# Seventeen weight sums from VectorE to GpSimd, with a new hand-written order, in a one-core attention and MLP kernel

## The chip, the cores and the metric

The kernel runs on one core of one Trainium2 chip. The metric is the device time of one execution in microseconds; lower is better. Five engines work beside each other, each through its own queue in order: TensorE (PE; its weight loads are listed as PEld), VectorE (DVE), ScalarE (ACT), GpSimd (POOL) and SyncE (SP), which here issues nearly all DMAs. An engine waits at the head of its queue until the semaphores of its next instruction are met, and everything behind that instruction waits too.

## The reference

Gated linear attention over four sequences of 768 tokens, eight heads of 48, and behind it one MLP block with a layer norm and a residual:

```python
def _attn_ref(q, k, v, alpha):            # (B, H, S, D) = (4, 8, 768, 48)
    for t in range(S):
        state = alpha[:, :, t, :, None] * state + np.einsum('bhd,bhe->bhde', k[:, :, t], v[:, :, t])
        y[:, :, t] = np.einsum('bhd,bhde->bhe', q[:, :, t], state)

def _moe_ref(x, g_ln, w_ch1, w_ch2):      # x is (4, 768, 384), w_ch1 (384, 1536), w_ch2 (1536, 384)
    xn = (x - mu) / np.sqrt(var + 1e-06) * g_ln
    return x + np.maximum(xn @ w_ch1, 0.0) @ w_ch2
```

All is computed in float32; the two weight matrices arrive as 64-bit floats and are turned into float32 on the chip.

## The kernel before

**Tiling.** The 768 tokens are cut into six chunks of 128, with the four sequences beside each other: 24 pieces of attention, each a generator `attention(c, b)`. Chunk 0 goes through the MLP in the plain way: `hidden` (line 561) and `project` (line 573). Chunks 1 to 5 use fast matrix multiplication. The first product xn @ w_ch1 is split into 3 x 3 blocks of the weights and 3 x 2 blocks of the tokens and made from 15 block products instead of 18 (`hidden_product`, line 853); the second from 20 instead of 24 (`product`, line 673). Each block product multiplies a sum of weight blocks by a sum of token blocks. The token side is summed once a chunk (`combine_x`, line 827; `combine_hidden`, line 660), the weight side once in all: `combine_first` for the first weights (line 802, the subject here) and `combine_weights` for the second (line 633).

**Order.** Nothing is scheduled automatically. Every part of the work is a Python generator, named by one character, and the string `ORDER` (lines 28 to 48, 1501 characters) says whose next step is emitted:

```python
for turn in ORDER:
    next(turns[turn], None)
```

Since each engine runs its queue in order, `ORDER` fixes on each engine what stands behind what. The characters that matter here: `a` to `x` are the 24 attention pieces (`a` is chunk 0, sequence 0); `0` to `3` issue the loads of alpha, k, q and v on SP; `A` to `L` load and convert the twelve weight pieces; `Y`, `Z`, `P`, `Q` are the MLP of chunk 0; `S` is `combine_first` (26 turns), `W` `combine_weights`, `X` `combine_x`, `N` `combine_hidden`, `M` and `V` the block products, `R` the relus, `O` the reloads of what is added at the end.

**combine_first.** Its first nine turns scale nine of the twelve blocks of w1 by the layer norm's gain, on ScalarE (line 779). Then follow 17 sums and differences of blocks, 17 turns, made with `add` and `sub` of line 786. A block is 128 x 512 float32. Two of the results are held as two halves of 128 x 256 in spare room, so these two take two instructions each, and two more halves make 19 instructions: 15 of 128 x 512 and 4 of 128 x 256. Results go to `ready`, from which `hidden_product` takes its weights; the block products of a chunk go in the order `FIRST = (11, 3, 7, 5, 10, 9, 1, 4, 14, 6, 13, 2, 8, 0, 12)`, and the first of them needs the twelfth of the 17 sums.

**What else stands on DVE and GpSimd.** On DVE: the conversion of weights (lines 223 to 233, with line 229 on ScalarE), q and k times their decay (line 309; the q form reads two SBUF tiles, the k form one SBUF tile and PSUM), masks (line 380), state updates (line 409), sums of the second weights (line 633), of tokens (827) and hidden blocks (660), and the sums that take block products out of PSUM (863 to 896 and 683 to 731). On GpSimd: causal masks of chunk 0 (line 377), the gate on the state (line 411, which follows line 409 and is waited for by the attention outputs of line 437), and late sums of the two fast products (lines 872, 875, 878, 879, 888, 891, 892, and 689).

**Attention's start.** A piece takes the logarithm of alpha (line 293, ScalarE), sums it with a triangular matmul (298, or 522 for later chunks), takes exponentials (303, 304), multiplies q and k (309), transposes them (325 or 346), and goes on to scores (366, 538), state updates (396) and outputs (421, 437); then come the norm (453 to 480) and its transposes (487, 503).

Of the kernel before, what the change touches and what calls it, by code (L numbers as in the profile page):

```python
# [25 lines left out]


ORDER = (
    "0aa0bb00c2211dd2a3a2aabbbcaaacbbb0bd1a1abbbdfa1dddaaa3bbbec4aac2cd0baaafdAcbe2cc"
    "ffebdddccccdebb31eg0abhAffffeeecA4gdddccA5fdggheddeeeccYYiYhBjfcfhdgeeecggdchhhg"  # L30
    "hBB1ZZZfffB3CCZAefffe5hghB4fCjYYYYYiZZZCYYZZDD2jji3YYiDjjjhiiEZZZC0kDYYY3hhhZEig"
    "FFE5iggjGlF4ZZZZZgglS1lEHYYYhhghHjYYGYYhZZ2llgll3jHZFYGjHkkZkgI0kk0kjjjYZZnKI3i3"
    "ImQSSiiGii4n2jj1jSj5IlkkkkJKSSSSl1feeJn2eKeJLLnhL0hi02jSmPSPSjjmmQ1PPKSSSPkffPP1"
    "fnhPhSmkSWWSQ2SmmSefefWgnggnhQphSogSilllS5n3mimnggXXlXXX33WQQQ0nnXQXk4ppXXomSlll"
    "lnMMpmMoonMMMMMM2MMWSSkk0XSXlmmnnnmmMmMMM3MM13MnMnooppMMMoMMMMWpkrRM0M5poqooo4iq"
    "WWjjMMMMiMMRWMMMpooRiRMMMWMMoMMMlMMOOM1rrr22MMMRRqipMpoiikWMMMMRRMRMMMnnppokMMMM"
    "MRRRNNp3nMONlNlp0nnpWOqtrrmmNWNrN0MMNMMMMMNkNMMMMNN3MMsMMMMMmq0pNlpq1q3kMNOMlkMN"
    "MMMM5XXXXXrrrqq4MqqNXt1XoMMMMMMXXsstqqproM2MrrrJMMuvpoMMMMMMXMMMMMMXsMMMMMtMMrMo"
    "stssMMMqMtMtMM52rrsttssm4ssstMRttMMMMtt1MrMOOMMMMrMvMO2MMMMRRRvRMMMMMMMRRMMRMMML"
    "u31uMMRMRMMssNqNNNvrsmu22RNNNNNRqqNNNNm001MpMMMMMMMMMMM3MMMMMMMMMMMMNMMMrppNoNuv"  # L40
    "vMMoMMMMMXXX3MMM1XXvuu5vuuXvwXXvx4twuuvvqqMXXOOuMMsttttOMMMMMMMMMMXMMMwtMMMMwMMM"
    "33txxxMMMMMMMRqMMMMMMMMMMMMMMMussMsruuwrxRRRMMMMMRRRMRxMMRMMMMwwMMMMMMvxvvvvv5xx"
    "xwwwwwNNRONRRNttqqMMNNxMMMMMxNvMMMMMMMMNNNNNwwxsvMvwwMMxsMMuNNMMXXxNNxxxXXMXXXMM"
    "MXMMMMMXOMMMxMMXXMMMMMMMMMMwwOOuMMMMMMMMMMMMMMMMMMMMMMMMMMMRRRMMMMMMMMMMMROMxwuR"
    "uuwMMMMMMMMMMRRRRNRMMRRMMNMNNMNNNNMMMMMMMMMMMxNMNNXXXXXXMMMXNNMMMMMMNNNMMVVVVVVX"
    "MMMXXXMMMMMMMMVVVVVVVVOOOMOVVVVVVVVVVVVVVVRRRRRVVVVVVVVVRVVVVVVVVVVVVVVVVVVVVVVR"
    "RRNNRNRMMNRNNNMMMNNNMMMMNNNMMMMMMMMMMMMMMMMMMMNNMMMMNMMMMMMMM"
)


# [1 line left out]
def kernel(  # L52
# [36 lines left out]
    nc = tc.nc  # L89
# [670 lines left out]
    def first_weights_ready():  # L760
        if "a" not in first_of:
            first_of["a"] = {n: [w1[:, 2 * t:2 * t + 2, f]]
                             for n, t, f in ((7, 2, 1), (10, 1, 0), (13, 0, 1), (8, 0, 0))}
        return first_of["a"]
# [11 lines left out]
    def combine_first():  # L776
        a = [[w1[:, 2 * t:2 * t + 2, f]] for t in range(3) for f in range(NF)]
        for n in (3, 7, 5, 8, 1, 4, 0, 2, 6):
            nc.scalar.mul(a[n][0], a[n][0], g_col[:, n % NF:n % NF + 1])
            yield  # L780
        extra = cpool.tile([P, 6 * P], FP32, name="extra")
        spare = [raw.tile([P, 2, 2, NP, D], FP32, name=f"r{n}", tag="in", bufs=6).rearrange(
            "t b i p d -> t (b i p d)") for n in "akq"] + [extra]
        n3, n5, n0, n11 = ([x[:, :4 * P].rearrange("p (a c) -> p a c", a=2)] for x in spare)
        n9, n1 = ([x[:, 4 * P:].unsqueeze(1) for x in spare[2 * i:2 * i + 2]] for i in range(2))
        add, sub = nc.vector.tensor_add, nc.vector.tensor_sub
        ready = first_weights_ready()

        def parts(x, n):
            return x if len(x) == n else [x[0][:, :1], x[0][:, 1:]]  # L790

        for n, op, out, x, y in (
                (3, sub, n3, a[3], a[7]), (5, add, n5, n3, a[5]), (9, add, n9, n3, a[8]),
                (None, sub, n0, a[1], a[3]), (1, sub, n1, n0, a[5]), (0, sub, n0, n0, a[4]),
                (None, sub, a[4], a[3], a[4]), (4, add, a[4], a[4], a[5]),
                (None, sub, a[5], a[0], a[7]), (None, sub, n11, a[2], a[8]),
                (14, add, a[8], a[5], a[8]), (11, sub, n11, n11, n5),
                (12, sub, a[5], a[5], a[6]), (None, sub, a[6], a[8], a[5]),
                (6, sub, a[6], a[6], a[7]), (None, add, a[2], a[2], a[0]),
                (2, sub, a[2], a[2], a[1])):  # L800
            for o, u, w in zip(out, parts(x, len(out)), parts(y, len(out))):
                op(o, u, w)
            if n is not None:
                ready[n] = out
            yield
# [117 lines left out]
    def second_of_chunk_0(h):  # L923
        for i in range(3):
            for b in range(2 * h, 2 * h + 2):
# [6 lines left out]
    turns |= {chr(ord("a") + n): attention(n // B, n % B) for n in range(NCB * B)}  # L932
    turns |= {chr(ord("A") + i): take_weights(i) for i in range(len(pieces))}
    turns |= {"M": mlp(), "V": hidden_products(NCB - 1), "S": combine_first(), "W": combine_weights(), "R": relus(),
              "X": (x for c in range(1, NCB) for x in combine_x(c)),
              "N": (x for c in range(1, NCB) for x in combine_hidden(c)), "O": outputs()}
# [32 lines left out]
```

## Time and profile before

| what | value |
|---|---|
| median of 3 runs | 425.02 us (424.80 to 425.43) |
| the profiled execution | 425.22 us |
| its span on the engines | 423.5 us |
| TensorE clock granted | 0.999 |
| GpSimd busy from 80 to 100 us, from 100 to 120 us | 2.03 us, 1.91 us |
| DVE busy in the same stretches | 18.15 us, 18.54 us |
| DVE busy from 400 to 420 us | 15.17 us |

The span is what the engines' records cover; the 1.7 us that the execution took beyond it lie around it. A row of a source view gives the line, engine, operation, tiles and count, then the shortest, median and longest duration in ns, the first and last start in us, and the shapes. A row of the view of waits reads: who waited and for whom, then us in total, how often, and the longest. A piece of the chain of waits gives its start, its length and what it was; matmuls are counted there by records, and a float32 matmul leaves two.

### The profile page before, as it was taken

The page shows a single profiled execution, that of the slowest core. Times are in us where ns is not written, and L with a number is a line of the kernel's source. Part 1 is how long each engine was busy: PE and PEld are TensorE (multiplying, and loading weights), DVE is VectorE, ACT ScalarE, POOL GpSimd, SP SyncE. Part 2 cuts the span into 40 slices and gives each one's busy share as a digit, 9 for nine tenths or more (in the row PEclk, how much of TensorE's full clock was granted, in tenths as well). Part 3 has the DMA queues.
Part 4 walks back from the last instruction along what each step waited for, and adds up shares of the span by engine and source line. Part 5 has one row for each costly group of instructions (what it writes and reads, how often), then busy time and mean ns, then how long its engine had stood idle before and what let it go on. Part 6 is the DMA issues. An engine that isn't in the chain of part 4 may idle for free.

```text
span 423.5 us, 14136 instructions
## 1 busy us (share of the span) xinstructions
PE 416.2 (98%) x5988; PEld 366.9 (87%) x5988; DVE 327.2 (77%) x626; ACT 228.1 (54%) x572; POOL 155.0 (37%) x181
## 2 busy tenths in 40 slices
PE   8989999999999999999999999999999999999997
PEld 6878778766778889998889998899998899988996
DVE  4688889898998988878678667749676679756684
ACT  6986577969634879434666066486432551114200
POOL 3242010110125491244771333771145650656414
PEclk9999999999999999999999999999999999999999
DMA  7989766783534341161513226002122000130001
GB/s 241 245 199 285 252 167 197 235 248 116 116 96 134 97 131 60 36 176 38 137 36 104 68 83 165 2 22 39 35 83 74 2 2 0 39 112 2 0 18 58
DMA packets 51095, 43.95 MB, mean 104 GB/s; under 512 B 23468, under 2 KB 47148, under 8 KB 51032
## 3 DMA queue, kind: packets, MB, share of 16 engines
q1 hardware_dynamic: 50632, 43.04, 35.5%
q8 instruction: 47, 0.77, 0.8%
q14 instruction: 16, 0.13, 0.1%
q10 hardware_dynamic: 400, 0.00, 0.1%
HBM read 34.29 MB, written 8.74 MB: 102 GB/s over the span
## 4 chain that ended last, share of the span: by engine, by line
PE 89%; ACT 3%; DVE 3%; DMA 2%; issue 1%; SPq 1%; DVEq 0%; ACTq 0%
PE ops L673 31%; PE hps L853 31%; PE ops L573 7%; PE hps L561 6%; PE yps L437 5%; PE aps L538 2%; PE tps L346 2%; PE ups L396 2%; DMA vx<-in_v_dram 1%; PE lps L522 1%; DMA ra<-in_alpha_dram 1%; PE tps L325 1%; PE xps L503 1%; DVE qk L309 1%; ACT qT L332 1%
## 5 line engine op out<-in xcount | busy, mean ns | idle before, releaser
L689 POOL TENSOR_TENSOR ob<-ob,u 128x192 f32<-128x192 f32 x40 | 25.4, 646 | 88.4 <-DVE ob L686 66.1
L853 PE MATMUL hps<-sum,w 128*128 128x256 f32 x192 | 47.5, 382 | 0.1
L411 POOL TENSOR_TENSOR mid<-mid,gate 112x192 f32<-112x192 f32 x20 | 11.4, 571 | 91.9 <-DVE mid L409 55.7
L853 PEld LDWEIGHTS hps<-sum,w 128*128 128x128 f32 x192 | 36.1, 190 | 5.1 <-DVE qk L309 0.2
L673 PE MATMUL ops<-w,hT 128*128 128x192 f32 x224 | 39.9, 327 | 0.0
L673 PEld LDWEIGHTS ops<-w,hT 128*128 128x128 f32 x224 | 36.9, 190 | 0.3
L561 PE MATMUL hps<-xT,w 128*128 128x256 f32 x144 | 33.5, 385 | 1.0 <-issue 0.9
L853 PE MATMUL hps<-xT,w 128*128 128x256 f32 x136 | 34.4, 380 | 0.0
L561 PEld LDWEIGHTS hps<-xT,w 128*128 128x128 f32 x144 | 26.6, 190 | 6.3 <-ACT lps L304 1.1
L573 PE MATMUL ops<-w,hT 128*128 128x384 f32 x96 | 32.0, 488 | 0.0
L904 ACT ACTIVATE hT<-hT 128x512 f32<-128x512 f32 x48 | 27.3, 628 | 7.9 <-POOL hT L891 2.7
L853 PEld LDWEIGHTS hps<-xT,w 128*128 128x128 f32 x136 | 25.8, 190 | 3.5
L673 PE MATMUL ops<-ws,sum 128*128 128x192 f32 x160 | 28.6, 327 | 0.0
L573 PEld LDWEIGHTS ops<-w,hT 128*128 128x128 f32 x96 | 17.9, 190 | 11.5
L683 DVE TENSOR_TENSOR ob<-ops,ob 128x192 f32<-128x192 f32 x50 | 17.1, 352 | 13.0 <-PE ops L673 7.6
L673 PEld LDWEIGHTS ops<-ws,sum 128*128 128x128 f32 x160 | 26.4, 190 | 0.0
L356 ACT COPY qT<-tps 112x512 uint16<-112x512 uint16 x32 | 17.2, 602 | 16.1 <-PE tps L346 16.0
L673 PE MATMUL ops<-ws,hT 128*128 128x192 f32 x128 | 23.4, 326 | 0.0
L507 ACT COPY xT<-xps 128x384 uint16<-128x384 uint16 x32 | 13.5, 492 | 16.9 <-PE xps L503 16.9
L673 PE MATMUL ops<-more,sum 128*128 128x192 f32 x120 | 22.2, 328 | 0.0
L673 PEld LDWEIGHTS ops<-ws,hT 128*128 128x128 f32 x128 | 21.3, 190 | 0.1
L437 PE MATMUL yps<-mid,qT 48*64 48x48 f32 x320 | 21.0, 220 | 0.0
(253 smaller groups left out, 1139.8 us busy)
## 6 DMA issues: line engine op xcount, KB each, us to landing
ws<-in_moe_w_ch_dram SPq DMA_DIRECT2D x12, 768.0 KB
vn<-in_v_dram SPq DMA_DIRECT2D x12, 384.0 KB
kept<-x SPq DMA_DIRECT2D x20, 192.0 KB
ob<-kept SPq DMA_DIRECT2D x20, 192.0 KB
out_dram<-ob SPq DMA_DIRECT2D x19, 192.0 KB
ra<-in_alpha_dram SPq DMA_DIRECT2D x18, 192.0 KB
rq<-in_q_dram SPq DMA_DIRECT2D x16, 192.0 KB
rk<-in_k_dram SPq DMA_DIRECT2D x16, 192.0 KB
```

The lines of the kernel that those rows point to most:

```text
L346: nc.tensor.transpose(tv[cs, n, p, w], words[halves[h], n, p, i, :cs.stop - cs.start, w], ident_of_halves[halves[h]])
L356: nc.scalar.copy(out=to, in_=tps[h].bitcast(UINT16).rearrange("r (n p w t) -> r n p t w", n=2, p=NP, w=2)[:R, n])
L411: nc.gpsimd.tensor_mul(new, new, by)
L437: nc.tensor.matmul(yps[r][halves[s], i, p], of, by, start=not (odd and inner), stop=bool(inner or not odd), skip_group_check=bool(odd))
L507: nc.scalar.copy(out=xT_of[c][:, :, b, halves[h]].bitcast(UINT16).rearrange("r f (t w) -> r f t w", w=2), in_=xps[h].bitcast(UINT16)[:, :2 ...
L561: nc.tensor.matmul(hps, w1[:, j // 2, f, j % 2 * P:][:, :P], xT_of[0][:, f, bs], start=(f == 0), stop=(f == NF - 1))
L573: nc.tensor.matmul(ops_of[b], hT_of[c][:, j, b], w2[:, j], start=(j == 0), stop=(j == NJ - 1))
L673: nc.tensor.matmul(acc, lhs[:, j], rhs[:, j], start=(j == 0), stop=(j == NT - 1))
L683: nc.vector.tensor_add(x, acc, x)
L689: getattr(nc.gpsimd, f"tensor_{op}")(x, x, y)
L853: nc.tensor.matmul(acc[:, i], w, b, start=True, stop=True)
L904: nc.scalar.activation(out=x, in_=x, func=AFT.Relu)
```

## The change

In `combine_first` the two operations of line 786 are taken from GpSimd instead of VectorE; all 17 sums, 19 instructions, follow. `ORDER` is replaced as a whole: the same 1501 characters in another sequence, with every generator taking as many turns as before. TensorE's 3742 matmul instructions are the same ones in another order.

```diff
 ORDER = (
-    "0aa0bb00c2211dd2a3a2aabbbcaaacbbb0bd1a1abbbdfa1dddaaa3bbbec4aac2cd0baaafdAcbe2cc"
+    "0aa000bcbca2211d0aabdcaaabbbdba3fbbeaa122bb4ccaade1aa1dbbbfaccccad2ddedabbf3bcAc"
...
-    "fnhPhSmkSWWSQ2SmmSefefWgnggnhQphSogSilllS5n3mimnggXXlXXX33WQQQ0nnXQXk4ppXXomSlll"
-    "lnMMpmMoonMMMMMM2MMWSSkk0XSXlmmnnnmmMmMMM3MM13MnMnooppMMMoMMMMWpkrRM0M5poqooo4iq"
+    "memmhPWSSWffQ0g2gWQWi0mn5ngnim3hgQSSghX1XSSSlXXX2XXXXQQQmlnllnnmXlnlpo4pop1loMol"
+    "MMSlSMMMMMMkjjSSMMMpjjMmmMMMSkkjpXmmjMMW3W3ppMMMmmMooMMRMoMMMMnnmnn5ooooMM0MMMnn"
...
 )

-        add, sub = nc.vector.tensor_add, nc.vector.tensor_sub
+        add, sub = nc.gpsimd.tensor_add, nc.gpsimd.tensor_sub
         ready = first_weights_ready()
```

The other lines of `ORDER` differ as much. In the new order the first seven of the 19 instructions stand on GpSimd behind the state update of st_0_105, the next seven behind one more update, then come three updates and four sums around the update of st_0_109, and the last stands behind the first sums of the fast product (lines 872 and 875). On ScalarE the first exponential (line 303) now stands behind the third logarithm (line 293), where before it stood behind the fourth.

More of the change, by code (lines that the diff above doesn't have):

```diff
@@ L28 @@
 ORDER = (
-    "0aa0bb00c2211dd2a3a2aabbbcaaacbbb0bd1a1abbbdfa1dddaaa3bbbec4aac2cd0baaafdAcbe2cc"
[L30 to L33, printed above, removed]
-    "fnhPhSmkSWWSQ2SmmSefefWgnggnhQphSogSilllS5n3mimnggXXlXXX33WQQQ0nnXQXk4ppXXomSlll"
@@ L35 @@
-    "lnMMpmMoonMMMMMM2MMWSSkk0XSXlmmnnnmmMmMMM3MM13MnMnooppMMMoMMMMWpkrRM0M5poqooo4iq"
[L36 to L46, printed above, removed]
@@ L47 @@
-    "RRNNRNRMMNRNNNMMMNNNMMMMNNNMMMMMMMMMMMMMMMMMMMNNMMMMNMMMMMMMM"
+    "0aa000bcbca2211d0aabdcaaabbbdba3fbbeaa122bb4ccaade1aa1dbbbfaccccad2ddedabbf3bcAc"
+    "daa3ffedeAbaeefffdeccccbAAcd0dgh5fcdfbdbccffeed4gede321BggdYcYYc0hggdghhhfgfhhhC"
+    "dZZBBBiZffj5f24eeeifZ1ZZZCjCCYYACYYYjBjhD33eeYYiiZZYgDj0ZDDiZhijij1EEZZZFEZYYZ5j"
+    "jhhhlYkEgg2gGYYFFYYihh4lhhkhGHlHl3ggZZ0ZZ0ZZGnYljYmiFijkgliHlZZYjkYSjjYYISSIgkkk"
+    "QiHKg4i3I3GjIjj13S5eke22SkeelkkJnhJKJLLK1hhmffffSSiQnLSSnSgWSSSSPKPP1kkePPWPPmnn"
@@ new lines @@
+    "memmhPWSSWffQ0g2gWQWi0mn5ngnim3hgQSSghX1XSSSlXXX2XXXXQQQmlnllnnmXlnlpo4pop1loMol"
+    "MMSlSMMMMMMkjjSSMMMpjjMmmMMMSkkjpXmmjMMW3W3ppMMMmmMooMMRMoMMMMnnmnn5ooooMM0MMMnn"
+    "npWWMMMpooMMMMMMWMMMMMMMMRRRMnMMMkR3kkppppr0q4ooJMOMRRrqRMrRiiONOMRMMM1RiiqMMOMM"
+    "k2rp0tMMNNNN0opNiinsoWrnRMppMMNrNr22qllMM2WNNMMNM3pNMMMMM1MlMlMppqllqkM0mqN0NpMM"
+    "MMM5k333NrN1rOqqrXXX4ttotXqMMXXrMM2qoqXXsMMMMXXMXMMMMMMrMMMMMMMMMMMrrMR1MssMqMMM"
+    "rrqtstMrMtrsMMMMMs5tsRttutv41uuvssvsssR00vMMMMMRRRrMMMMMM2utsMMMMMMRMMMMMMRsq22p"
@@ new lines @@
+    "pMMRMMRMMMqMMMNRNNMOOMOrrNNNoRNMMMsssmM3x3mMsMMsMNNNNNNMMMMqMMMMwMMMNMMMMMMttMmo"
+    "uovvvMMmMNNMMMuuM1MM1XXX5vtuuXuXXXtX4xvvvvqqMXOXMMuuMxxwwMOXttqtMMMMMMMMMMMMMMMM"
+    "MMMMMMMMMOMRRRRMMMMwMMMMMMMMMMMMuurrxwwxRxMMMMMRMR3MMRMRMMMMMMMw5xxtvtuvxxxvRRwu"
+    "vuwwN3wNtsNMsMMMMNNNONNRvMMvMMMMMvNNNtNMMMxxMwwvwqMMMNvXqXXMMNXXXXXXXXMMNMNMMMMM"
+    "MMMMMMMMMMMMMMMMMMMMMMMMMMMMMMMMMMuxwwwwMMMMMxMMMMMRRRRRMMMMMMMMMRMMMROMOMMMMMMM"
+    "MMMMMRRMOORRRxxxMNMNNNMMMMMMMNNMNNNxxuwwMXuXXXXXXMMMXXXXMMMMMNNNVVMVVNVMVVVVMMNM"
@@ L48 @@
+    "MMMMMMNNMMMMMMMOOMOMOLVVVVVVVVVVVVVVRVRRVVRVVVVVVVVVRVVVVVVVVVVVVVVVVVVVRVVVVVVR"
+    "RRNNNNRRNMMMMNRNNMNNMMNNNMMMMMMMMMMMMMMMMMMNMNNMMMMMMMMMMMMMM"
 )
```

## The prediction

> **What bounds the kernel now.** I read the busy shares first, then the chain of waits by engine, then the waits of TensorE alone, and last the groups that the change touches.
>
> ```profile
> PE 416.2 (98%) x5988; PEld 366.9 (87%) x5988; DVE 327.2 (77%) x626; ACT 228.1 (54%) x572; POOL 155.0 (37%) x181
> ...
> PE 89%; ACT 3%; DVE 3%; DMA 2%; issue 1%; SPq 1%; DVEq 0%; ACTq 0%
> ```
>
> TensorE is busy for 416.2 of 423.5 us and has 89% of the chain that ends last: there is little but its own work. The view of its waits names what it lost to others:
>
> ```profile
> PE lps L250 <- DVE small L251: 1.1, 1, 1.1
> PE xps L487 <- ACT la L293: 1.1, 1, 1.1
> PE hps L561 <- issue: 0.9, 1, 0.9
> PE xps L503 <- DVE hT L881: 0.4, 1, 0.4
> PE yps L437 <- DMA vx<-in_v_dram: 0.2, 1, 0.2
> PE tps L325 <- DVE qk L309: 0.2, 1, 0.2
> ```
>
> 3.9 us in all. The first is the start and stays; 2.8 us could go. They stand at 23.0 (L487), 44.5 (L561), 153 (L503) and 38.8 us (L437). Whatever DVE is spared, no more than these 2.8 us and something in the first 8 us can come back. The removed work, in the view of line 802, and the row that prices it on GpSimd, in the view of line 872:
>
> ```profile
> L802 DVE TENSOR_TENSOR w<-w x9: 682/686/692, 104.8 to 129.6; 128x512 f32<-128x512 f32 x9
> L802 DVE TENSOR_TENSOR extra<-rq,w x1: 419/419/419, 102.0 to 102.0; 128x256 f32<-128x256 f32 x1
> ...
> L872 POOL TENSOR_TENSOR hT<-hT,u x8: 1270/1276/1390, 131.5 to 334.8; 128x512 f32<-128x512 f32 x8
> ```
>
> None of the rows of line 802 has anyone waiting for it.
>
> **The moved instructions.** 19 instructions: 15 on 128x512 and four on 128x256. DVE loses 15 x 0.686 + 4 x 0.42 = 12.0 us. On GpSimd a 128x512 addition takes 1.27 us; 128x256 is not shown, so I interpolate between 0.590 (128x192, line 689's median) and 1.27: 0.59 + 64/320 x 0.68 = 0.73 us (bounds 0.59 and 1.27). GpSimd gains 15 x 1.27 + 4 x 0.73 = 22.0 us on 155.0. It is nearly idle where they go: 2.03 us busy from 80 to 100 us and 1.91 from 100 to 120.
>
> **Do they arrive in time?** By the built program's order the first seven stand after the state update st_0_105 (line 411), seven more after one further update, four around st_0_109 shortly ahead of the first product, and the last behind line 875. The first product (11) needs the fourteenth. TensorE reaches it at 121.7 us, while the scaled blocks are there from about 98 us as before; two groups of 6.7 and 8.9 us and an update of 0.51 end near 115: 6 us to spare. Product 6 needs the four: 4 x 1.27 + 0.51 = 5.6 us of queue, against 10.6 us of TensorE work between their place and product 6 (its pitches added up): 5 us to spare. Product 2 needs the last: behind product 4 come line 874 (0.69), line 875 (1.27) and the addition (1.27), 3.2 us, against 6.2 us of TensorE work: 3 us. Queued behind them on GpSimd are the updates of line 411 that gate the attention outputs (line 437) and the late sums of the hidden blocks (lines 872 to 892); these are shifted by at most 1.27 us after the last. I cost the move itself at 0; if that 3 us cover were gone, one addition, 1.27 us.
>
> **What GpSimd does to DVE.** The trace shows that an addition on GpSimd can stop DVE. In the view of line 309 and in the time lines of DVE and GpSimd:
>
> ```profile
> L309 DVE TENSOR_TENSOR qk<-rq,eq x20: 546/553/1874, 7.1 to 266.9; 128x384 f32<-128x384 f32 x20
> ...
> 150.94 1.87 DVE L309 TENSOR_TENSOR qk<-rq,eq 128x384 f32<-128x384 f32 x1
> ...
> 151.13 1.27 POOL L878 TENSOR_TENSOR hT<-u 128x512 f32<-128x512 f32 x1
> ```
>
> The product of two SBUF tiles took 1.87 us instead of 0.55 while an addition of 1.27 ran on GpSimd: it waited 1.32. The other form of line 309, which reads PSUM (qk<-rk,lps), never went above 0.555. Some ten DVE instructions with two SBUF inputs (lines 225, 231, 233, 633, 309, 827) fall beside the moved ones. Each can lose from 0 to 1.32 us; line 827's 0.42 has a longest of 1.017. That is 0 to 13 us on DVE; I take a third, 4 us, because most DVE rows of these lines stay at their median. DVE still ends 8 us lighter. On TensorE only the few whose result is due at once count: around the first products line 309's q half stands directly behind the sum that releases line 872, and the transposes of line 346 follow within 2 us of TensorE work. I take one such wait: 0.4 us, as L503 lost at 153, bounds 0 and 2 x 1.32 = 2.6.
>
> The Trainium skill, "SBUF — State Buffer", section "Who interferes with whom", speaks against the change: VectorE instructions with two SBUF inputs and GpSimd share one port pair under an exclusive lock, so the later one fully blocks. The 1.87 agrees. By that rule all ten meetings would cost a whole addition, 13 us on DVE, more than the 12.0 spared; by the rows' mean it is 4.
>
> **The new sequence on TensorE.** Both programs have 3742 matmul instructions in 140 stretches of one line. Heavy stretches (lines 561, 573, 673, 853) go from 40 to 43, light ones from 100 to 97. Entering a stretch is priced from the chain:
>
> ```profile
> 130.02 3.65 PE hps L853 x16
> ...
> 315.80 21.58 PE hps L853 x100
> ```
>
> (21.58 - 3.65)/84 = 0.2135 us a record, so 3.65 - 16 x 0.2135 = 0.23 us for the entry. For line 437, 64 records take 1.08 and 128 take 2.01: entry 0.15. So 3 x 0.23 - 3 x 0.15 = +0.25 us (-0.4 to +0.7).
>
> **Its start.** Before, ScalarE takes four logarithms ahead of the first exponential; the fourth waits for a load until 6.16 us, the exponential starts at 6.59, DVE's product at 7.09, the transposes at 7.80. Now the exponential stands ahead of the fourth logarithm and can start at 5.42: up to 1.17 us earlier. But the transposes of k need the first k load: issued at 3.60, and with the 3.96 us of the alpha load in the chain it lands near 7.56, against 7.94 where its product started. I take -0.4 (-1.17 to 0). Behind it two loads of 384 KB in all (alpha of chunk 1) now precede the v load; that is due only near 12 us.
>
> **The waits.** At 23.0: L487 waited 1.1 for normalised rows that stood behind four products on DVE (the last took 1.01) beside a GpSimd select; now only one of the four is between. I take -0.8 (-1.1 to 0). At 38.8: the v exchange load stands two weight loads earlier in SP's queue: -0.2. At 153: its cause was the collision above, and DVE is lighter there: -0.4. At 44.5: cause not shown, 0 (-0.9 to 0).
>
> **Sum.** 0 + 0.4 + 0.25 - 0.4 - 0.8 - 0.2 - 0.4 = -1.15 us. The profiled execution took 425.22 us: 423.5 of span and 1.7 around it; it would be 424.1. It lies 0.2 above the median of 425.02, so the median goes to 423.9.
>
> **The rivals.** *Collisions decide.* The q products of line 309 meet the additions near the first products, TensorE waits in line 346 for a whole blocked instruction twice (2.6 us instead of 0.4), and the early waits stay: -1.15 + 2.2 + 0.8 = +1.85, and 426.9. It decides once a blocked product ends after TensorE has come to its transposes. For it: the 1.87 row. Against: DVE has 8 us less to do.
> *The first weights are late.* GpSimd's updates of line 411 wait for DVE, the additions behind them start over 3 us late, and products 6 and 2 wait 1.27 each: 423.9 + 2.5 = 426.4. For it: the queue is in order, and line 411 idles 55.7 us for line 409. Against: the 3 to 6 us to spare.
> *The waits only move.* DVE's load was no limit and the new order gives back what it takes: 425.0. For it: of the 2.8 us only 0.4 is put down to DVE's hT.
> *All of it goes.* -1.17 - 2.8 + 0.25 = -3.7: 421.3. For it: DVE is about 90% busy from 20 to 160 us. Against: L561's wait was for no one shown.
>
> **How the numbers follow.** Forecast 0.40; all of it goes 0.12; the waits only move 0.14; collisions 0.26; late weights 0.08. What counts as no change is within 0.2%, 0.85 us, about what a measurement can tell. Faster 0.52, same 0.14, slower 0.34. The forecast's own range is 422.9 to 424.6. The whole range, 421.2 to 427.5, takes in all the rivals' times; its upper end adds 0.6 to 426.9 for a third collision partly hidden.
>
> **What would show it.** Right: 19 rows of line 802 on POOL, 1.27 and about 0.73 us, DVE near 319 us busy, POOL near 177; first transposes before 7.8; no TensorE wait for POOL w. Wrong: a TensorE wait above 1 us in L346 or L853 near 120 to 135 us, or more than 2.8 us of new waits before 60 us.

## The result, and the profile after

| | before | after |
|---|---|---|
| median (lowest to highest) | 424.98 us (424.28 to 427.76, 8 runs) | 428.35 us (426.94 to 429.58, 8 runs) |
| ratio, 95% interval | 1 | 1.0062 [1.0033, 1.0091] |
| profiled execution | 425.22 us | 427.89 us |
| its span | 423.5 us | 426.2 us |

The changed kernel is slower by 0.6%, some 2.6 us by the ratio, in which the two kernels ran beside each other (the medians of the table differ by 3.4). The forecast was 423.9 and the range ended at 427.5. The busy shares of the page after:

```profile
PE 417.2 (98%) x5988; PEld 367.4 (86%) x5988; DVE 320.4 (75%) x607; ACT 229.4 (54%) x572; POOL 185.5 (44%) x200
```

The 19 instructions are where they should be: DVE has 19 fewer and POOL 19 more. But DVE should have come to 327.2 - 12.0 = 315.2 and has 320.4; POOL should have come to 177.0 and has 185.5. Both engines lost time that the profile counts as work: 5.2 and 8.5 us. (About 3 of the 8.5 are not the sums' doing: the new order without them, measured below, has POOL at 158.0.) TensorE's waits, by whom it waited for (us in total, times, longest):

```profile
PE ops L573 <- DVE x L456: 1.1, 1, 1.1
PE lps L250 <- DVE more L247: 1.1, 1, 1.1
PE tps L325 <- DVE more L309: 1.1, 1, 1.1
PE tps L325 <- DVE qk L309: 1.1, 2, 0.7
PE lps L298 <- ACT la L293: 0.9, 2, 0.6
PE aps L366 <- issue: 0.2, 1, 0.2
PE hps L853 <- issue: 0.2, 1, 0.2
```

The four old waits that were to go (lines 487, 561, 503, 437) are indeed gone. In their place stand 4.6 us of others: 5.7 in all against 3.9. With 1.0 us more of TensorE's own time that is, to 0.1 us, the 2.7 by which the span grew. There are two scenes. The first, in the time lines of DVE (start, length, instruction), POOL and TensorE:

```profile
84.36 2.38 DVE L233 SCALAR_TENSOR_TENSOR w<-w,ws 128x768 f32<-128x768 f32 x1
86.67 0.55 DVE L456 SCALAR_TENSOR_TENSOR x<-yps,x 128x384 f32<-128x384 f32 x1
...
90.62 1.50 DVE L227 TENSOR_SCALAR ws<-ws 128x768 int32<-128x768 int32 x1
```

```profile
83.54 1.15 POOL L411 TENSOR_TENSOR st<-st,gate 112x192 f32<-112x192 f32 x1 [3.21 <-DVE st L409]
84.65 1.28 POOL L802 TENSOR_TENSOR ra<-w 128x512 f32<-128x512 f32 x1
86.01 1.86 POOL L802 TENSOR_TENSOR rk<-ra,w 128x512 f32<-128x512 f32 x1
```

```profile
87.27 2.20 PE L573 MATMUL ops<-w,hT 128*128 128x384 f32 x6 [1.14 <-DVE x L456]
```

The last step of a weight conversion (line 233, two SBUF inputs, median 0.96 us) took 2.38 us. It stood still for the end of line 411's update and the whole first sum on GpSimd; line 456 stands behind it, and TensorE's line 573 waited for line 456 until 87.27. The second sum in turn took 1.86 instead of 1.27: the engines stop each other. Line 227, with a single SBUF input and a median of 0.565, took 1.50 beside the sums that follow.

The second scene is the start, in SP's queue:

```profile
14.44 0.47 SPq L211 DMA_DIRECT2D ws<-in_moe_w_ch_dram  x1
19.41 0.37 SPq L157 DMA_DIRECT2D vn<-in_v_dram  x1
19.88 1.10 SPq L313 DMA_DIRECT2D row<-eq  x2
21.03 0.92 SPq L386 DMA_DIRECT2D gate<-row  x2
22.06 1.35 SPq L147 DMA_DIRECT2D ra<-in_alpha_dram  x2
```

From 14.9 to 19.4 us nothing is issued: the third load of v waits for one of its two buffers, and rows, gates and the alpha of chunk 1 wait behind it. Before, that alpha stood ahead of the weight load:

```profile
14.20 1.52 SPq L147 DMA_DIRECT2D ra<-in_alpha_dram  x2
```

The logarithms, exponentials and k products that need it come late, and TensorE waits in line 325 at 34.7 us (1.1) and 36.5 us (0.4). The third wait of this line, 0.7 us at 9.7, stands ahead of all this.

### The profile page after: what moved, and what is told of

Its sections match the earlier page's. It is cut to its first block, busy times and chain, and to the rows that moved or that the text cites. A ratio compares the mean times of both kernels' runs of the same rounds, so it can differ in the third digit from the quotient of the medians.

```text
span 426.2 us, 14127 instructions
## 1 busy us (share of the span) xinstructions
PE 417.2 (98%) x5988; PEld 367.4 (86%) x5988; DVE 320.4 (75%) x607; ACT 229.4 (54%) x572; POOL 185.5 (44%) x200
## 5 line engine op out<-in xcount | busy, mean ns | idle before, releaser
L904 ACT ACTIVATE hT<-hT 128x512 f32<-128x512 f32 x48 | 28.6, 633 | 25.7 <-POOL hT L875 14.4
L411 POOL TENSOR_TENSOR mid<-mid,gate 112x192 f32<-112x192 f32 x20 | 12.9, 650 | 44.3 <-DVE mid L409 33.1
L872 POOL TENSOR_TENSOR hT<-hT,u 128x512 f32<-128x512 f32 x8 | 11.1, 1387 | 27.3 <-DVE u L871 27.3
L437 PEld LDWEIGHTS yps<-st,qT 48*64 48x64 f32 x320 | 18.4, 134 | 4.7 <-issue 2.4
L411 POOL TENSOR_TENSOR st<-st,gate 112x192 f32<-112x192 f32 x16 | 11.0, 685 | 23.5 <-DVE st L409 20.8
```

What stands on the lines that cost most here:

```text
L411: nc.gpsimd.tensor_mul(new, new, by)
L437: nc.tensor.matmul(yps[r][halves[s], i, p], of, by, start=not (odd and inner), stop=bool(inner or not odd), skip_group_check=bool(odd))
L872: add_late(c4, c4, u2)
L904: nc.scalar.activation(out=x, in_=x, func=AFT.Relu)
```

## The experiments

Sixteen kernels ran, each beside the kernel before on the same chip. Ratios are to that kernel, with 95% intervals.

### The two halves of the change by themselves

`order_alone` has the new `ORDER` and the sums on VectorE; `engine_alone` the old `ORDER` and the sums on GpSimd:

```diff
 # engine_alone, in combine_first
-        add, sub = nc.vector.tensor_add, nc.vector.tensor_sub
+        add, sub = nc.gpsimd.tensor_add, nc.gpsimd.tensor_sub
```

> The new sequence with the 17 sums back on VectorE. Theory A (two causes: the sequence loses about 1.3 us in the first 45 us, and blocked VectorE instructions lose 1.1 us at 87 us): 426.4 us, the 2.38 us row of line 233 near 84 us back at 0.96, TensorE behind the old kernel by 1.2 to 1.9 us at the same work near 40 us. Theory B (the sequence alone): 428.3. Theory C (GpSimd's additions alone): 425.0.

> The old sequence with the 17 sums on GpSimd. Theory A: 425.0 to 427.0, by where the additions meet VectorE's two-input instructions in that sequence; VectorE busy about 5 us more than 327.2 - 12.0 = 315.2. Theory B: 425.0. Theory C: 428.3.

Measured: order_alone 432.61 us, 1.0164 [1.0126, 1.0201]; engine_alone 436.87 us, 1.0264 [1.0228, 1.0300]. Each half alone is far worse than both together, and neither number was expected. The trace of order_alone is of its longest execution, 437.08 us, so it shows where this kernel can lose time and not what its median lost. In it VectorE is busy for 14.86 of the 15 us from 100 to 115, among them the sums, and TensorE waits for it later, 2.4 us in line 522 at 129 us; 5.2 us of other waits stand before 60 us. The view of waits of engine_alone:

```profile
PE ops L573 <- DVE w L233: 7.1, 2, 5.5
PE hps L853 <- DVE qk L309: 1.4, 1, 1.4
```

and its DVE time line, whose rows normally take 0.55, 0.96, 0.57 and 0.96 us:

```profile
95.43 2.08 DVE L223 TENSOR_SCALAR w<-ws 128x768 int32<-128x768 int32 x1
97.55 1.91 DVE L225 SCALAR_TENSOR_TENSOR w<-ws,w 128x768 f32<-128x768 uint32 x1
99.49 1.51 DVE L227 TENSOR_SCALAR ws<-ws 128x768 int32<-128x768 int32 x1
...
104.52 1.90 DVE L233 SCALAR_TENSOR_TENSOR w<-w,ws 128x768 f32<-128x768 f32 x1
```

From 86 to 106 us GpSimd runs sum after sum, and each of these steps loses 0.9 to 1.5 us, where a sum alone takes 1.27. Line 573 needs the converted block and gets it at 106.48. So the "move itself, costed at 0" had a price of its own that depends on what DVE does at that moment: in the old order it is the conversion that TensorE needs next.

### Without the sums

In the next two the 17 sums are left out, and the products read scaled blocks in their place.

```diff
-            for o, u, w in zip(out, parts(x, len(out)), parts(y, len(out))):
-                op(o, u, w)
             if n is not None:
-                ready[n] = out
+                ready[n] = parts(next(t for t in a if len(t) <= len(out)), len(out))
```

> The old sequence with the 17 sums left out (19 instructions on no engine; the products of the weights read scaled blocks in their place, so the output differs). It shows what the relief of VectorE is worth by itself where GpSimd disturbs nobody. Theory A (the 11 us of the moved sums in the old sequence are blocked conversions): line 233's longest stays near 0.96 to 1.15 us, TensorE's 7.1 us of waits in line 573 are gone, the time is 422.5 to 425, at or under the kernel before. Rival B (the sums come too late on GpSimd for the products, or the change of DVE's load upsets this sequence): the time stays above 428.

> The new sequence with the 17 sums left out in the same way. Against the changed kernel (428.35) it gives the whole price of the collisions in the new sequence. Theory A (about 1 us of collision, the wait in line 573; the rest is the start and the order): 426.5 to 427.5, with the start's waits in line 325 unchanged. Rival B (the collisions are all of the loss): 424 to 425.5. Rival C (they cost nothing): 428.3.

Measured: 424.25 us, 0.9981 [0.9957, 1.0005], in the old order; 426.87 us, 1.0038 [1.0013, 1.0063], in the new one. In both, theory A's range held. The row of line 233 in old_seq_no_sums (shortest, median, longest in ns) shows that nothing is held up any more:

```profile
L233 DVE SCALAR_TENSOR_TENSOR w<-w,ws x12: 957/959/1144, 30.4 to 98.6; 128x768 f32<-128x768 f32 x12
```

and in new_seq_no_sums, at the place of the first scene:

```profile
84.28 1.14 DVE L233 SCALAR_TENSOR_TENSOR w<-w,ws 128x768 f32<-128x768 f32 x1
85.47 0.56 DVE L456 SCALAR_TENSOR_TENSOR x<-yps,x 128x384 f32<-128x384 f32 x1
```

The wait in line 573 is gone there and those in line 325 (0.7 and 0.8) stay. All six cells, as ratios:

| | no sums | sums on VectorE | sums on GpSimd |
|---|---|---|---|
| old order | 0.9981 | 1 | 1.0264 |
| new order | 1.0038 | 1.0164 | 1.0062 |

Read along the rows: where VectorE makes the sums, they cost 0.0019, that is 0.8 us, in the old order and 0.0126, 5.4 us, in the new one. On GpSimd they cost 12 us in the old and 1.0 us in the new one. Each order suits one engine. Read down the first column: the new order by itself, with no sum anywhere, costs 0.0057, 2.4 us. From before to after: -0.8 (the work gone from VectorE) + 2.4 (the order) + 1.0 (what the sums on GpSimd cost in it) = +2.6 us. By the runs' intervals the first term is good to about 1 us and the other two, differences of two ratios, to about 1.5: the order's 2.4 is told from zero, the -0.8 and the +1.0 are not. That the sums hold up TensorE in the new order is seen in the trace, in line 573's wait; what they cost in time is not measured to better than that.

### Fewer sums on GpSimd

`five_on_vector` keeps the first five sums (seven instructions, those at 84 to 93 us) on VectorE, in the new order. `old_seq_last5` has only the last five on GpSimd, in the old order. Both in the form

```diff
-                op(o, u, w)
+                getattr(nc.vector if k < 5 else nc.gpsimd, f"tensor_{op}")(o, u, w)
```

with `k` the number of the sum, and 12 in place of 5 in the second.

> The changed kernel with the first five of the 17 sums (seven instructions) back on VectorE, the same sequence. Theory A (the additions that follow each other on GpSimd at 84 to 88 us hold up the weight conversions of lines 223 to 233 on VectorE, and line 573 waits for what stands behind them): line 233's longest falls from 2.4 us to about 0.96, TensorE's wait of 1.1 us in line 573 is gone, the time falls by about 1 us to 427.3. Rival B (VectorE has too much to do here, whatever GpSimd does): 4.4 us more on VectorE at 84 to 90 us make the wait in line 573 longer, by up to 4 us, and the time is 429 to 432.

> The kernel before, its sequence untouched, with only the last five of the 17 sums on GpSimd, which stand behind all conversions of the first weights. Theory A (the 11 us that the whole move costs in the old sequence come from blocked conversions of lines 223 to 233 alone): the time of the kernel before within 1 us, and line 233 at 0.96 us throughout. Rival B (every sum on GpSimd costs VectorE or TensorE about the same, 11 us for 19 instructions): five instructions cost 2.9 us, some 428.5.

five_on_vector: 428.44 us, 1.0083 [1.0052, 1.0113]. Line 233's longest fell to 1.15 and the wait in line 573 went, as theory A had it; the time did not fall. New waits stand at 107 and 125 us (1.0 in line 346 and 0.7 in line 853, both for line 309): the sums' 3.7 us on VectorE, from 100 to 104 us, stand ahead of the q product that the first one waits for. The second is not explained by them: the rows of DVE's time line around it are those of the changed kernel, 0.5 us later. Both theories were half right. VectorE, 14.9 of 15 us busy from 95 to 110 us here, has little room for the sums.

old_seq_last5: 426.21 us, 1.0040 [1.0015, 1.0066], by the ratio 1.7 us worse than before and past theory A's 1 us, though its interval begins at 0.6. The conversions are untouched, but another instruction was caught, in the DVE time line:

```profile
119.53 2.71 DVE L827 TENSOR_TENSOR sum<-sum,xT 128x256 f32<-128x256 f32 x1
122.16 0.54 DVE L309 TENSOR_TENSOR qk<-rk,lps 128x384 f32<-128x384 f32 x1
```

and POOL's:

```profile
119.47 3.90 POOL L802 TENSOR_TENSOR w<-w 128x512 f32<-128x512 f32 x3
```

A sum of tokens that takes 0.42 us alone took 2.71: it stood still for two sums that followed each other. Line 309 is behind it, and TensorE waited 1.4 us in line 853. So it is not the conversions as such: another DVE instruction with two SBUF inputs that stands ahead of something due can be the victim.

### The start

`old_start` is the changed kernel with the first 235 turns (up to about 60 us) in the old order; `new_start` the kernel before with its first 235 turns in the new one.

```diff
+ORDER = OLD[:235] + (what is left of NEW, in its order)    # old_start
```

> The changed kernel with the first 235 turns of the old sequence, and behind them the new one's remaining turns in its order. Theory A: the start's 1.3 us come back, 427.0, with the wait of line 573 near 87 us still there. Theory C: 428.3. Theory B with all its loss in the start: 425.6.

> The kernel before (sums on VectorE) with the first 235 turns of the new sequence and then the old one's. Theory A: 426.3 us, all of it lost before 45 us. Theory C: 425.0.

Measured: old_start 426.76 us, 1.0028 [1.0006, 1.0049]; new_start 427.97 us, 1.0061 [1.0032, 1.0091]. The start's order accounts for 1.4 us on one side and 2.6 on the other, about all of the 2.4 that the new order costs without sums. The 2.6 is told from zero; the 1.4, a difference of two ratios that is good to about 1.5, is not quite. The traces point the same way: line 573's first matmul starts at 80.2, 80.3 and 80.3 us in the changed kernel, new_seq_no_sums and five_on_vector, and at 77.8 and 79.0 in old_start and old_start_five, whose turns between the start and there are the same. (These are single executions; in the four traces that have the old order throughout it starts between 77.0 and 80.0.) `old_start_five`, old_start with the first five sums on VectorE as well, was to beat it:

> The changed kernel with the first 235 turns in the old order and the first five sums on VectorE: both suspected losses are taken out. If they are separate and add up: the 1.6 us that the old start brought (426.76 against 428.35) and about 1 us more, 425.5 to 426, which is the time of the kernel before. If the collisions of the five sums cost nothing: 426.8. If VectorE is the bound there: 428 or more.

It came to 426.73 us, 1.0045 [1.0022, 1.0068]: no gain, for the reason seen in five_on_vector (line 346 waits 1.1 us for a q product).

Which part of the start? Seven runs took it apart, after the picture of SP's blocked queue. In `load_first` the alpha load (`0`) goes ahead of the v load (`3`):

```diff
-...bcAcdaa3ffedeAbaeefffdeccccbAAcd0dgh...
+...bcAcdaa03ffedeAbaeefffdeccccbAAcddgh...
```

> The changed kernel with one turn moved: the load of alpha's chunk 1 for k stands ahead of the third load of v instead of behind it. Theory A (the loss at the start is SP's queue, which stands still from 14.9 to 19.4 us because the third v load waits for a buffer, with the alpha load behind it): the alpha load is issued near 15 us instead of 22, TensorE's two waits in line 325 at 34.7 and 36.5 us (1.1 and 1.1 in the view of waits) are gone, and the time falls by 1 to 2 us against the changed kernel, to 426.4 to 427.4. Rival B (the start is late because two alpha loads stand ahead of the first v load, which this kernel leaves as it is): no change, 428.3.

428.86 us, 1.0091 [1.0056, 1.0125]: no gain. The alpha was issued at 14.03 and line 325's waits shrank from 2.2 to 0.3 us, but others came:

```profile
PE aps L538 <- issue: 1.8, 1, 1.8
PE aps L538 <- DVE xT L490: 1.6, 1, 1.6
PE ups L396 <- issue: 1.3, 1, 1.3
```

DVE's time line of the same run says why:

```profile
23.08 0.78 DVE L223 TENSOR_SCALAR w<-ws 128x768 int32<-128x768 int32 x1 [2.31 <-DMA ws<-in_moe_w_ch_dram]
...
26.07 0.54 DVE L490 TENSOR_TENSOR xT<-xps,small 128x384 f32<-128x384 f32 x1
```

The first weight block now lands at 23.1 instead of 22.0 us, and its conversion stands at the head of DVE's queue ahead of what TensorE needs. In the old order, line 490 stands ahead of it. So the following runs moved that conversion to a later place (`load_and_later`: its first step on DVE, with the alpha load as in load_first; `conv_late`: its steps on DVE and ScalarE alone; `alpha_conv_late`: these and the alpha load ahead of the weight load), or took the v load from the head of the queue (`swap_v_alpha`: exchanged with the alpha load; `v_later`: moved behind it), or put only the first 50 turns in the old order (`old_first_50`).

> The changed kernel with the alpha load of chunk 1 moved ahead of the third v load, as in the run load_first, and besides the first conversion of weights (lines 223 to 227 on VectorE) put behind the copy of line 490 and the next row of line 476 instead of ahead of them. Theory A (in the new start VectorE's queue stands still for a weight load of 768 KB that lands at 22 to 23 us, and what TensorE needs next stands behind it): the wait of 1.6 us in line 538 at 26.8 us that load_first showed is gone, so are those in line 325, and the time is 426.5 to 427.5. Rival B (the new start is slow because of its first 12 us): 428.3 or more.

> The same without moving the alpha load: the first weight block is loaded as early as in the changed kernel, only its steps on VectorE and ScalarE stand later. Theory A: the two logarithms still wait for the alpha load, which is issued near 22 us, so TensorE's waits in line 325 near 35 us stay and the time is 428 to 429. If the time is 426.5 to 427.2 as well, the load's place was no part of the loss, only the conversion's.

> The changed kernel with three things at its start put as the old order has them: the alpha load of chunk 1 (m = 1) ahead of the first weight load, the first conversion on VectorE (lines 223 to 227) behind the copy of line 490 and the next row of line 476, and ScalarE's step of that conversion (line 229) behind the two logarithms of line 293 instead of ahead of them. Theory A (the new start loses because the first weight block's load and conversion stand ahead of attention's steps in three in-order queues): no wait of TensorE above 1 us from 20 to 45 us, the start gives back what the old start did, 426.5 to 427.2. Rival B (the loss is spread over the whole start and comes back elsewhere whatever is moved): 428.3 or more, with a new wait above 1 us before 50 us.

> The changed kernel with two turns exchanged: the alpha load of chunk 1 (m = 1) takes the place of the third v load, and the third v load takes its place. SP's queue then has no instruction that waits for a v buffer ahead of the rows, the gates and the alpha load. Theory A (the new start loses by the v load that stands still at the head of SP's queue): alpha is issued near 15 us, the rows and gates of the second pair at 16 to 19 us instead of 19.9 to 21.9, TensorE's waits in line 325 near 35 us are gone without a new one above 1 us, and the time is 426.4 to 427.2. Rival B (the start has no slack, and any moved load meets the next wait): 428.3 or more, with a new wait above 1 us before 50 us.

> The changed kernel with the third v load alone moved, to right behind the alpha load of chunk 1. Theory A: the rows and gates are issued at 16 to 19 us, alpha right behind them near 18 us instead of 22.06, the waits in line 325 shrink from 1.8 us in all to under 0.5, and the time is 426.4 to 427.2. Rival B: 428.3 or more.

> The changed kernel with only the first 50 turns in the old order, that is the loads and products of the first some 10 us, and all others in the new one. Theory A (the loss of the new start comes from 14 to 37 us: late alpha, the conversion of weights at the head of VectorE's queue): 428 or more, the waits in line 325 at about 35 us stay. Rival B (it comes from the first loads, alpha of chunk 1 ahead of v): 426.8, as with the first 235 turns.

| run | median, us | ratio, 95% interval | longest new wait of TensorE before 50 us |
|---|---|---|---|
| load_and_later | 432.23 | 1.0164 [1.0129, 1.0199] | 2.3, line 522 for line 293, whose logarithms stand behind line 229 on ScalarE |
| conv_late | 430.37 | 1.0132 [1.0102, 1.0161] | 2.2, line 561 for line 233 |
| alpha_conv_late | 431.63 | 1.0146 [1.0121, 1.0172] | 2.2, line 561 for line 233 |
| swap_v_alpha | 428.92 | 1.0100 [1.0069, 1.0131] | 1.6, line 538 for line 490 |
| v_later | 430.46 | 1.0118 [1.0087, 1.0148] | 1.6, line 396; 1.5, line 538 |
| old_first_50 | 431.66 | 1.0122 [1.0079, 1.0165] | 2.0, line 522 for line 293 |

The gain that theory A promised failed to come in load_first, load_and_later, alpha_conv_late, swap_v_alpha and v_later, and conv_late was slower than it allowed. In one run or another the alpha came early, the queue of SP ran on, or the conversion stood later, and every time the next thing was late, the weights themselves among them. old_first_50 shows that the old order of the first 10 us, put ahead of the new rest, does not help; but its wait of 2.0 us, at 14.6 us in line 522, is in neither kernel, so it does not clear those 10 us. Rival B of the last runs, that this start has no slack and any moved turn meets the next wait, fits all seven, though only alpha_conv_late, swap_v_alpha and v_later recorded it in this form. That the start as a whole costs something near 2 us is shown; that one load or one conversion is its cause is not, and it stays open whether a single one is.

## Why the prediction was wrong

*The sign came from the terms for the order, and they failed.* The sum put the new sequence at +0.25, its start at -0.4 and the early waits at -0.8, -0.2 and -0.4: -1.55 us together. The new order without any sums measured +2.4 us. The error lies in three places of that working.
- "Its start: -0.4." The first exponential was to start at 5.42; it started at 6.32, as the third logarithm waited for its load until 5.89, and the first product at 7.39 then waited for q. The first transposes came at 8.4 us, not before 7.8. The two alpha loads that "now precede the v load" were noted, and what they and the v load do to SP's queue was not followed past 12 us: the third v load and what stands behind it were not listed.
- "The waits." Each of the four named waits went, and I booked them as gains without asking which instructions had taken their places. Sparing a wait in a kernel whose TensorE is 98% busy is worth something only if nothing else is as late; here 4.6 us of new waits came. Nor was one trace enough to price them: in the five other traces that have the old start (engine_alone, old_seq_no_sums, old_seq_last5, old_start, old_start_five) the wait in line 487, booked at -0.8, is 1.1, 2.6, 0.3, 0.5 and 0.6 us, and that in line 561, before 60 us, is 0.3, none, 0.3, 0.2 and 0.6. Apart from the first wait, which stays, TensorE's waits before 60 us come to 1.0 to 3.4 us in the six traces with the old start and to 2.3 to 3.3 in the changed kernel, new_seq_no_sums, new_start and five_on_vector.
- "The new sequence on TensorE." TensorE's own time grew by 1.0 instead of 0.25 us, and why stays open. Line 522 grew most, from 9.14 to 9.89 us, but it has 9.68 in old_seq_no_sums, where its order is the old one.

The rows of ScalarE on which the -0.4 failed:

```profile
5.89 0.52 ACT L293 ACTIVATE la<-ra 128x384 f32<-128x384 f32 x1 [1.28 <-DMA ra<-in_alpha_dram]
6.32 0.47 ACT L303 ACTIVATE eq<-lps 128x384 f32<-128x384 f32 x1
```

*The collisions: right mechanism, size within its bounds, wrong place.* +0.4 (0 to 2.6) was to come near the first products at 120 to 135 us, from line 309. It measured +1.0 us, good to about 1.5, and the wait that the trace shows stands at 86 to 87 us, behind line 233, 35 us earlier than where I looked. The prediction took the scaled blocks to be there "from about 98 us as before". Before, the last block is scaled at 97.6 us; the first ones are there earlier, and in engine_alone, with the old order, GpSimd starts its first sum at 84.5. The sums start as soon as GpSimd is free and their blocks are there, not where the products need them. "A third of 13 us" on DVE measured 5.2, put together otherwise: not ten rows that lose 0.4 each, but six from 84 to 136 us (lines 233, 225, 227 and three of 633) that took 0.4 to 1.4 longer than their medians, 0.9 on average. The third had no row behind it. The sentence from the Trainium skill, "SBUF — State Buffer", section "Who interferes with whom" (the loser blocks for the whole instruction), gave 13, and engine_alone has 329.9 - 315.2 = 14.7 us on DVE. That the totals are near is luck: there fifteen rows lost 0.4 to 2.3 us, 0.9 on average, not ten a whole sum of 1.27 or more each. The same section also names single-input forms that can take the shared pair; I had counted only those with two inputs, and lines 223 and 227 at 2.08 and 1.50 us agree with the page.

*The move at 0.* No wait for POOL's w appeared, so the slack to products 11, 6 and 2 was judged rightly, and the rival of late first weights fell. But the relief of VectorE, from which the lighter DVE was to follow, is worth 0.8 us even if the work vanishes (0.9981, in an interval that holds 1). That ceiling was in the profile of before: no row of line 802 had anyone waiting for it.

*The rivals.* Two had the sign: "collisions decide", 426.9, came nearest to the measured time, though its early waits did not stay and its place was another. The true cause, an order that makes more waits than it takes away, was closest to "the waits only move", and that rival was priced at 425.0 on the assumption that an order gives back no more than it takes.

*What would have shown it.* "More than 2.8 us of new waits before 60 us" was the right alarm: 3.1 us stand there in lines 325 and 298 alone, against 0.2 before.

## What to carry to other kernels

Before moving elementwise work to GpSimd, measure the ceiling by leaving the work out: here 0.8 us, against a price of 12 us in one order and about 1 in the other, by which DVE instruction happens to be running. Look for the victims where GpSimd will start, not where the result is due, and at what stands behind each victim in DVE's queue. A hand-written order is tuned to its engines as a whole: judge a new one by listing, for each in-order queue, the first instruction that will wait and everything behind it, and expect that moving one turn of it can uncover the next wait. Price a wait from several executions: here one wait of the same order went from 0.3 to 2.6 us.

## What the runs showed of the hardware

**A wait of TensorE can cost more than its length.** In engine_alone the view of windows (window, its length; then busy us and count of PE, PEld, DVE, ACT, POOL; granted clock, DMA share, GB/s) reads:

```profile
98.00:102.00 4.00, 2.99 (x10) 1.45 (x8) 3.97 (x3) 0.97 (x2) 3.84 (x3) 1.00 0.00 0
102.00:106.00 4.00, 0.00 (x0) 0.00 (x0) 3.96 (x3) 3.84 (x14) 3.92 (x4) 0.93 0.18 50
106.00:108.00 2.00, 1.52 (x3) 0.92 (x4) 1.97 (x3) 1.87 (x7) 1.55 (x1) 0.50 0.33 98
...
110.00:112.00 2.00, 2.00 (x5) 1.09 (x4) 0.00 (x0) 0.51 (x1) 0.00 (x0) 0.50 0.44 128
112.00:114.00 2.00, 2.00 (x80) 1.09 (x81) 0.51 (x2) 0.00 (x0) 0.00 (x0) 0.94 0.19 69
```

The clock falls in the last half microsecond or so before 106 us, near the end of 5.5 us of waiting, and is back soon after 112: some 7 us at half. TensorE works for 5.8 of these, and half of that, 2.9 us, is lost by it: about a quarter of the 12 us that the kernel lost. (Its busy time is 3.6 us longer in all, 419.8 against 416.2.) Shorter waits can do it too. In v_later one wait of 1.5 us in line 538 (TensorE busy for 2.47 of the 4 us from 40 to 44) is followed by

```profile
44.00:46.00 2.00, 2.00 (x11) 0.74 (x3) 0.95 (x2) 0.72 (x2) 0.00 (x0) 0.50 0.94 340
```

while in swap_v_alpha waits of 1.3 and 1.6 us in the same line left the clock at 1.00. The mean granted clock of an execution goes in steps: order_alone's executions had 1.000 (430.34 us), 0.996 (431.77, median of two), 0.992 (433.44, median of two) and 0.988 (437.08). A step of 0.004 is 0.004 x 427 = 1.7 us, one stretch of 3.4 us at half clock. So load_and_later, at 0.992 in five of six executions, lost two such stretches, 3.4 us, that the view of waits does not show; in its trace the clock is 0.57, 0.50, 0.50 and 0.72 in the four windows of 2 us from 32 to 40 us. This is also a good part of what sets the slower ones of the seven runs apart: executions at 1.000 took 426.87 to 430.4 us in load_first, swap_v_alpha, v_later, conv_late and old_first_50, and 426.94 to 428.9 in the changed kernel. The Trainium skill, "TensorE: Matmul & The Clock Gate", Part 1, says that the clock is halved after an idle window of some 3.4 us. The half agrees; but here stretches in which TensorE was partly busy were enough, and the 3.4 us worked out above is how long a half clock lasted, not how long TensorE was idle.

**DVE can be stopped for more than one instruction of GpSimd.** 2.38 and 2.71 us (lines 233 and 827) are longer than the victim alone (0.96 and 0.42) and one sum of 1.27 us together: line 233 waited through the end of an update and a whole sum, line 827 through two sums. And sums of 128x512 took up to 2.00 us on GpSimd beside DVE, 1.27 alone.
